# RetNet attention and a SwiGLU FFN on one core: eight attention jobs ahead of all up groups, and two token units that share each rounded weight group

## The chip, the cores and the metric

One core of a Trainium2 chip runs one program. The time is device microseconds (us) of one execution. The kernel before was run again beside each group of experiments and had medians of 1198.7 to 1199.44 us, so medians of different groups can be set side by side. A ratio is the mean time of one kernel's runs over that of the other's of the same rounds, so it is not quite the ratio of the medians that are quoted.

## The reference

Eight sequences of 576 positions, eight heads of 64, go through a retention layer. Its output is the input of an FFN over 4608 tokens. The FFN's weights come as float64.

```python
# attention: q, k, v are (8, 8, 576, 64) float32
scores = scale * np.matmul(q, k.transpose(0, 1, 3, 2))
Dmat = np.where(rel >= 0, gamma[:, None, None] ** rel[None, :, :], 0.0)
attn = np.matmul(scores * Dmat[None, :, :, :], v)
# FFN: x is (4608, 512), w_gate and w_val (512, 1536), w_out (1536, 512)
rms = np.sqrt(np.mean(x * x, axis=-1, keepdims=True) + 1e-06)
xn = x / rms * rms_g
g = xn @ w_gate
out = (g * (1.0 / (1.0 + np.exp(-g))) * (xn @ w_val)) @ w_out
```

## The kernel before

The attention is cut into 32 jobs, one for two heads of one sequence. First q and k of a job are turned, that is, transposed; the 64 positions left over after four blocks of 128 are its tail. TensorE then makes scores and states of a job, VectorE weighs them and sums the states, TensorE makes the values and the part carried over from earlier chunks, and VectorE moves the result into `x`. The FFN works on units of 384 tokens. Of each unit the squares of `x` are summed and averaged and `x` is scaled (the norm), then come the up groups (`w_gate` and `w_val`), then the down projection (`w_out`). The first two units use plain products and the other ten a scheme with fewer multiplications; those ten take most of the time, and the change does not touch them.

The weights are rounded from float64 to float32 on the chip, in 18 chunks of 1 MB. One chunk costs VectorE five instructions and ScalarE three:

```python
def exponent(i):                 # VectorE, then three Relu on ScalarE
    nc.vector.tensor_scalar(out=e, in0=words_of[i][..., 1::2], scalar1=20, ...)
    nc.scalar.activation(out=e.bitcast(F32), in_=e, func=AF.Relu, bias=least)
    ...                          # two more
def mantissa(i):                 # three on VectorE; the third needs e
    ...
def join(i):                     # one on VectorE
    ...
def weights_to(n):               # before: one chunk at a time
    while n_chunks < min(n, len(chunks)):
        mantissa(n_chunks + 1)
        join(n_chunks)
        load_chunks(n_chunks + 4)
        exponent(n_chunks + 2)
        n_chunks += 1
```

The order of the start is what the change is about. The jobs of sequence 0 (0 to 3) are turned by TensorE. The jobs of sequence 1 (4 to 7) are turned by VectorE and stand between the up groups of unit 0. An up group is a pair `(m, g)`: `m` says gate or value, `g` which third of the width; it takes two chunks of weights and is made of four quarters of about 2.6 us.

```python
for j in range(NHP):             # jobs of sequence 0
    slot(j)                      # scores, states, weigh; values and carried of job j - 1
    if j + 1 < NHP:
        turn(j + 1)
    ...                          # a chunk rounded at j == 1 and at j == 2
...
order = [(0, 0, 0), 4, (0, 1, 0), 5, (0, 0, 1), 6, (0, 1, 1), 7, (0, 0, 2)]
order += [(1, 0, 0), (1, 1, 0), (0, 1, 2)]
order += [(1, m, g) for g in (1, 2) for m in range(2)]
for what in order:               # (unit, m, g), or a job of sequence 1
    ...
    weights_to(4 * g + 2 * m + 2)
    for _ in up_plain(u, m, g):
        step += 1
        weights_to(2 + (step + 1) // 2)
```

## Time and profile before

| | us |
|---|---|
| median of 3 runs | 1199.05 (1198.05 to 1199.83) |
| first weighing of a job on VectorE | 18.48 |
| down projection of unit 1 starts on TensorE | 219.72 |
| from there to the end of the span | 981.3 |

The stages of the profiled span of 1201.0 us and the orders of time are in the prediction below. In a stage line the first number after the window is its length, then comes each engine's busy time with its count of instructions, then the clock granted to TensorE (1.00 is full speed), the share of the 16 DMA engines that was busy, and GB/s.

### The profile page before, as it was taken

To read this page: it belongs to the slowest core of one execution; us is meant where nothing else is said; L and a number is where in the kernel's file an instruction comes from. 1 tells how busy PE (TensorE), PEld (TensorE's weight loads), DVE (VectorE), ACT (ScalarE), POOL (GpSimd) and SP (SyncE) were. 2 spreads that over 40 slices of the span, in tenths; PEclk is the share of its full clock that TensorE was granted. 3 is DMA by queue.
4 is the path that set the end of the run, shared out by engine and by line. 5 is a ranking of instruction groups with operands and counts; after the bars stand their busy time and mean duration, and the time that the engine had idled before them with its cause. 6 is when DMAs were issued, how large, how long until landed. Compare 5 with 4: busy or idle time off the path is not lost.

```text
span 1201.0 us, 24041 instructions
## 1 busy us (share of the span) xinstructions
PE 1147.4 (96%) x10184; PEld 1036.7 (86%) x10184; DVE 674.6 (56%) x1370; ACT 244.3 (20%) x468; POOL 44.9 (4%) x74
## 2 busy tenths in 40 slices
PE   3798799999999999999999999999999999999998
PEld 3555455446999999999999999999999999999998
DVE  3888872024775666355566566446556555535442
ACT  4555541011220211220210211120220111120110
POOL 0000004130000000000000000000000000000000
PEclk9698799999999999999999999999999999999999
DMA  9498431021376455306436446405345412403304
GB/s 227 113 217 185 142 131 53 10 65 45 93 212 134 99 130 128 122 2 134 113 82 133 103 108 145 128 1 129 92 109 124 112 55 80 132 1 90 121 1 105
DMA packets 302347, 126.28 MB, mean 105 GB/s; under 512 B 279328, under 2 KB 284832, under 8 KB 302240
## 3 DMA queue, kind: packets, MB, share of 16 engines
q1 hardware_dynamic: 289840, 105.30, 36.5%
q10 hardware_dynamic: 12400, 19.44, 5.0%
q8 instruction: 80, 1.31, 0.5%
q14 instruction: 27, 0.22, 0.1%
HBM read 109.75 MB, written 14.94 MB: 104 GB/s over the span
## 4 chain that ended last, share of the span: by engine, by line
PE 82%; DVE 13%; issue 2%; ACT 1%; DMA 1%; SPq 0%; POOL 0%; DVEq 0%; ACTq 0%; POOLq 0%
PE x L438 13%; PE z L438 13%; PE w L438 13%; PE up L495 7%; PE wo L568 7%; PE y L438 6%; PE out L509 5%; PE xo L568 4%; PE zo L568 4%; PE yo L568 3%; DVE sum L282 2%; PE av L318 1%; DVE sq L378 1%; DVE ret L270 1%; DVE x L333 1%
## 5 line engine op out<-in xcount | busy, mean ns | idle before, releaser
L462 ACT COPY m<-x 128x384 f32<-128x384 f32 x60 | 28.7, 478 | 431.7 <-PE x L438 431.7
L438 PE MATMUL z<-x,w_gate 128*128 128x192 f32 x480 | 89.3, 330 | 2.2 <-DVE sum L282 2.2
L438 PE MATMUL x<-x,w_val 128*128 128x192 f32 x480 | 89.6, 330 | 0.0
L438 PE MATMUL x<-x,w_gate 128*128 128x192 f32 x480 | 88.8, 328 | 0.0
L438 PE MATMUL w<-sums,w_val 128*128 128x192 f32 x480 | 87.8, 326 | 0.0
L438 PE MATMUL z<-x,w_val 128*128 128x192 f32 x480 | 87.8, 326 | 0.0
L438 PE MATMUL w<-sums,w_gate 128*128 128x192 f32 x480 | 87.8, 326 | 0.0
L438 PEld LDWEIGHTS z<-x,w_gate 128*128 128x128 f32 x480 | 80.7, 192 | 2.5 <-DVE sum L282 2.5
L568 PE MATMUL xo<-h,w_out 128*128 128x192 f32 x480 | 82.1, 328 | 0.0
L568 PE MATMUL wo<-h,w_out 128*128 128x192 f32 x480 | 82.0, 328 | 0.0
L438 PEld LDWEIGHTS x<-x,w_val 128*128 128x128 f32 x480 | 79.8, 191 | 0.6
L438 PEld LDWEIGHTS x<-x,w_gate 128*128 128x128 f32 x480 | 79.7, 191 | 0.5
L438 PEld LDWEIGHTS w<-sums,w_gate 128*128 128x128 f32 x480 | 79.6, 190 | 0.0
L438 PEld LDWEIGHTS w<-sums,w_val 128*128 128x128 f32 x480 | 79.6, 190 | 0.0
L438 PEld LDWEIGHTS z<-x,w_val 128*128 128x128 f32 x480 | 79.6, 190 | 0.0
L568 PEld LDWEIGHTS xo<-h,w_out 128*128 128x128 f32 x480 | 78.1, 190 | 0.5
L568 PEld LDWEIGHTS wo<-h,w_out 128*128 128x128 f32 x480 | 78.1, 190 | 0.0
L445 DVE TENSOR_TENSOR u<-m,y 128x384 f32<-128x384 f32 x60 | 32.8, 546 | 79.8 <-PE y L438 79.8
L445 DVE TENSOR_TENSOR h<-u,w 128x384 f32<-128x384 f32 x60 | 33.3, 554 | 75.0 <-PE w L438 75.0
L495 PE MATMUL up<-x,w_gate 128*128 128x384 f32 x192 | 68.2, 515 | 4.0 <-DVE h L501 2.1
L495 PEld LDWEIGHTS up<-x,w_gate 128*128 128x128 f32 x192 | 38.2, 202 | 33.1 <-issue 3.6
L457 ACT ACTIVATE h<-h 128x384 f32<-128x384 f32 x90 | 47.0, 523 | 88.6 <-DVE h L445 88.6
(120 smaller groups left out, 1764.1 us busy)
## 6 DMA issues: line engine op xcount, KB each, us to landing
w_out<-w_blocks SPq DMA_DIRECT2D x70, 768.0 KB, 4.9
k<-in_k_dram SPq DMA_DIRECT2D x64, 128.0 KB, 3.1
v<-in_v_dram SPq DMA_DIRECT2D x64, 128.0 KB, 3.0
qraw<-in_q_dram SPq DMA_DIRECT2D x112, 72.0 KB, 2.7
kraw<-in_k_dram SPq DMA_DIRECT2D x112, 72.0 KB, 2.7
out_dram<-o SPq DMA_DIRECT2D x304, 24.0 KB, 1.6
w_out<-in_moe_w_gate_dram ACTq DMA_DIRECT2D x6, 1024.0 KB, 5.8
w_blocks<-w_out SPq DMA_DIRECT2D x7, 768.0 KB, 5.7
```

The source lines that it names most:

```text
L270: nc.vector.scalar_tensor_tensor(out=ret[:, e], in0=s[:, e, :SC].rearrange("p (c k) -> p c k", k=L), scalar=float(_gamma(H)[2 * hp + e] ** ...
L282: nc.vector.scalar_tensor_tensor(out=t[:, c], in0=t[:, c - 1], scalar=gc[:, hp : hp + 1], in1=part, op0=ALU.mult, op1=ALU.add,)
L318: mm = nc.tensor.matmul(av[odd][side(e), i * L : i * L + L], lhsT=d["sum"][side(e), c - 1], rhs=d["qT"][side(e), c * L : c * L + L], start ...
L333: nc.vector.tensor_tensor(out=x[:, first - c0 // L :: 2], in0=av[odd][:, i * L : (i + n) * L].rearrange("p (c k) -> p c k", k=L), in1=gq[: ...
L378: nc.vector.tensor_tensor(out=sq[a], in0=sq[a], in1=sq[b], op=ALU.add)
L438: nc.tensor.matmul(ps[:, i * HU : i * HU + HU], lhsT=w_up[m][:, 2 * blk + c, cut], rhs=t_of[u][blk][:, c], start=(start and i == c == 0), ...
L445: nc.vector.tensor_tensor(out=o, in0=a, in1=pairs_of(ps), op=ALU.add)
L457: nc.scalar.activation(out=o, in_=c, func=AF.Silu)
L462: nc.scalar.copy(out=s1, in_=pairs_of(x_))
L495: nc.tensor.matmul(ps[:, :U], lhsT=w_up[m][:, 4 * half + c, i * P : i * P + P], rhs=x_of[u][:, c], start=(c == 0), stop=(c == NHP - 1),)
L509: nc.tensor.matmul(ps[:, :DM], lhsT=h_of[u][:, f, s * P : s * P + P], rhs=w_out[:, f], start=(f == 0), stop=(f == NF - 1),)
L568: nc.tensor.matmul(ps[:, i * HU : i * HU + HU], lhsT=w_slots[:, k % 4, c, i * P : i * P + P], rhs=rhs[:, c], start=(start and i == c == 0) ...
```

## The change

The intent: do all eight jobs first, with TensorE turning all of them, and then let both units use a weight group one after the other, so that the rounding of two chunks has the products of two groups on TensorE to hide behind and not of one. The rounding is made a generator, of which one or two steps are taken at a time. Other parts: q comes in runs of 1 KB, the tails of all heads of a sequence in three loads, v is scaled by GpSimd, the Silu table is loaded at once, and the first four chunks are loaded by the sync queue.

```diff
@@ turn
-        scale_v(j)
+        for e in range(2):
+            for t in (d["v"][:, :, e], d["vt"][:, e].unsqueeze(1)):
+                g = gv[: t.shape[0], hp, e : e + 1].unsqueeze(2).to_broadcast(list(t.shape))
+                nc.gpsimd.tensor_tensor(out=t, in0=t, in1=g, op=ALU.mult)
@@ rounding, in steps (each yield ends one)
+    def rounding():
+        ...
+        exponent(0)
+        yield
+        exponent(1)
+        yield
+        yield from mantissa(0)
+        yield
+        for i in range(len(chunks)):
+            if i + 1 < len(chunks):
+                yield from mantissa(i + 1)
+                yield
+            join(i)
+            n_chunks += 1
+            load_chunks(i + 4)
+            yield
+            if i + 2 < len(chunks):
+                exponent(i + 2)
+                yield
@@ start
+        nc.scalar.activation(out=tick, in_=mhalf[:1], func=AF.Silu)
+        load_first(0)
+        load_tails(0)
+        load_first(1)
+        load_first(2)
+        load_chunks(1, nc.sync)
+        ... (tables, turn of job 0)
+        for j in range(2 * NHP):
+            slot(j)
+            if j + 1 < 2 * NHP:
+                turn(j + 1)
+            ... (squares, loads of job j + 2, norm of unit 0, loads of job 8 at j == 5 and 6)
+            load_chunks((1, 2, 2, 3, 3, 4, 4, 4)[j], nc.sync)
+            weights((0, 1, 2, 2, 2, 2, 1, 0)[j])
+        for m, g in [(m, g) for g in range(NG) for m in range(2)]:
+            for u in range(2):
+                weights_to(4 * g + 2 * m + 1)
+                for i, _ in enumerate(up_plain(u, m, g)):
+                    ... (values, carried and norm of unit 1 inside the first group)
+                    weights(2)
+                    if i == 1:
+                        weights_to(4 * g + 2 * m + 2)
+        following(2 * NHP - 1)
         weights_to(len(chunks))
```

## The prediction

> **What bounds the kernel now.** I first read the stages (busy time of each engine between chosen instants), then the order of time of TensorE and VectorE in the first 300 us, then the start on ScalarE. The stages:
>
> ```profile
> core 0: us, PE busy (x) PEld busy (x) DVE busy (x) ACT busy (x) POOL busy (x), PEclk, DMA share, GB/s
> 0.00:22.90 22.90, 9.29 (x210) 7.37 (x211) 4.44 (x18) 7.08 (x18) 0.78 (x7) 1.00 1.01 248
> 22.90:57.00 34.10, 21.14 (x405) 16.86 (x401) 27.81 (x69) 22.73 (x37) 1.13 (x4) 0.69 0.56 133
> 57.00:147.40 90.40, 74.83 (x728) 47.35 (x729) 78.38 (x136) 43.91 (x60) 1.21 (x5) 0.87 0.75 179
> 147.40:219.90 72.50, 72.50 (x225) 42.82 (x226) 34.26 (x43) 21.72 (x27) 15.96 (x12) 1.00 0.23 78
> 219.90:287.00 67.10, 67.10 (x364) 31.74 (x363) 9.93 (x25) 7.73 (x18) 16.10 (x14) 1.00 0.16 41
> 287.00:1201.00 914.00, 902.59 (x8263) 890.61 (x8260) 519.74 (x1083) 141.08 (x310) 9.67 (x32) 1.00 0.40 100
> ```
>
> From 147.4 us on TensorE is never idle except for some 11 us in 914; the change touches nothing there. Before it, TensorE waits: the start (22.9 us), the four jobs of sequence 0 at VectorE's pace (27.81 busy of 34.10), then weight rounding, the four jobs of sequence 1 and five of the twelve up groups, again with VectorE nearly full (78.38 of 90.40). So only the first 219.9 us can move. The other 979 us (1199.05 - 219.9) stay.
>
> TensorE shows what a wait costs and what an up group costs without waits:
>
> ```profile
> start us, us, engine line op out<-in xcount [idle before <-releaser]
> 102.65 0.37 PE L257 MATMUL last<-v,k 64*64 64x64 f32 x2 [3.75 <-ACT h L503]
> ...
> 104.77 12.04 PE L495 MATMUL up<-x,w_val 128*128 128x384 f32 x32
> ...
> 157.80 20.80 PE L495 MATMUL up<-x,w_val 128*128 128x384 f32 x64
> ```
>
> Two groups in 20.80 us, or 72.48 us for the seven from 147.4 to 219.9: 10.35 us a group, 2.59 a quarter of one. After a 3.75 us idle the same group takes 12.04.
>
> VectorE's units of work, from its order of time, are one job and one 1 MB weight chunk:
>
> ```profile
> 34.84 0.88 DVE L270 SCALAR_TENSOR_TENSOR ret<-s,causal 128x320 f32<-128x320 f32 x2
> 35.64 0.21 DVE L280 COPY sum<-s 128x64 f32<-128x64 f32 x1
> 35.89 1.86 DVE L282 SCALAR_TENSOR_TENSOR sum<-sum,gc,s 128x64 f32<-128x64 f32 x6
> 37.85 0.28 DVE L282 SCALAR_TENSOR_TENSOR sum<-sum,gc,last 128x64 f32<-128x64 f32 x1
> 38.05 0.94 DVE L333 TENSOR_TENSOR x<-av,gq 128x192 f32<-128x192 f32 x4
> 38.91 0.68 DVE L707 TENSOR_SCALAR w_val<-w_out 128x1024 uint32<-128x1024 uint32 x1
> 39.63 1.23 DVE L711 SCALAR_TENSOR_TENSOR w_val<-w_out,w_val 128x1024 f32<-128x1024 uint32 x1
> 40.77 1.22 DVE L714 SCALAR_TENSOR_TENSOR w_gate<-w_out,w_gate 128x1024 uint32<-128x1024 uint32 x1
> 41.91 1.22 DVE L722 SCALAR_TENSOR_TENSOR w_gate<-w_gate 128x1024 f32<-128x1024 f32 x1
> 43.16 0.69 DVE L686 TENSOR_SCALAR w_gate<-w_gate 128x1024 uint32<-128x1024 uint32 x1
> ...
> 184.29 1.58 DVE L722 SCALAR_TENSOR_TENSOR w_out<-w_out,w_gate 128x1024 f32<-128x1024 f32 x1
> ```
>
> By start-to-start: weighing a job 3.2 us (34.84 to 38.05), moving it into x 0.86; a chunk is 0.7 + 1.14 + 1.14 + 1.25 + 0.61, about 4.9. The last line is used below. The start on ScalarE:
>
> ```profile
> 13.57 1.28 ACT L199 ACT_TABLE_LOAD   x1 [13.57 <-DMA v<-in_v_dram]
> ```
>
> ScalarE issues the weight loads too; its queue stands until 13.57, so copies of turned q and k that could have begun at 10 to 11 begin at 14.86, and the first weighing at 18.48.
>
> **The Trainium skill.** (1) "TensorE: Matmul & The Clock Gate", Part 1: an idle window of about 3.4 us halves the clock, and about 3.4 us of sustained work restores it. The trace agrees: idles of 3.75 and 4.08 us are followed by a granted 0.50, one of 2.15 us is not. (2) "SBUF — State Buffer", Who interferes with whom: GpSimd and a VectorE instruction with two SBUF inputs exclude each other. The trace of before has one sign of it: the joining instruction takes 1.58 us at 184.29, beside GpSimd's work, and 1.22 elsewhere. (3) "ScalarE: Activation LUTs", What ACT_TABLE_LOAD costs: about 1283 ns for a load; here 1.28 us, twice (13.57 and 51.15). (4) "DMA: Bandwidth & Descriptors", Specifications: runs of at least 512 B for line rate. No row of the before trace isolates it; 2 us slices with weights alone in flight move up to 414 GB/s, slices with 64-float rows about 170.
>
> **The change part by part.**
>
> Start. q comes in runs of 1 KB, one load a job instead of three; the last 64 rows of all heads in three loads; weights are issued later and from the sync queue; the table is loaded at once. The built program gives eight completion semaphores to all loads in turn, so each load waits for the one eight before it: the tails of q and k go out at about 5 to 6 us (loads cost 0.5 to 0.6 us to issue, 2.4 to land unloaded, as q did at 4.07), land at 8.2, and turn, copy, scores and states (1.35 + 1.1 us at the slow clock) put the first weighing W0 at 11.4 instead of 18.48.
>
> Eight jobs. The four stream transposes of q and k of sequence 1 (2 x 0.7 us each job) leave VectorE, and TensorE turns them: about 1.6 us at full clock. v is scaled on GpSimd (estimate 2.1 us a job, from its 1.40 us for 128x512). VectorE carries 3.2 + 0.86 a job, 0.5 for the sum of squares, and ten rounding steps. TensorE's order, though, is a chain: states, carried (1.2), turn (1.6), the tail's two copies and turns behind each other on ScalarE (1.2), values (0.8; half waits for the last sum, because it takes over its bank), scores and states (1.3): 6.1 us a job. So a job takes the larger of 6.1 and VectorE's work. VectorE: job 1 4.7, 2 5.9, 3 6.85, 4 6.4, 5 8.25 (with the norm's 1.0 us wait for GpSimd), 6 7.3. I add 0.5 to 1 for jobs 2 to 6 for exclusion by GpSimd, 3.4 in all, and 6.5 for job 0 at the slow clock. W7 = 11.4 + 6.5 + 6.2 + 6.7 + 7.7 + 7.2 + 9.2 + 7.5 = 62.4.
>
> Between. The first quarter of the first up group hides behind the last weighing. Then values and carried of job 7 (to W7 + 5.5) and one quarter (to 8.1); the next needs chunk 1, which VectorE joins only after the last weighing, two moves and two sums of squares and four rounding steps: W7 + 12. A TensorE idle of 3.8 us. The two quarters after it, the mean and the scale of unit 1 bring its first group to W7 + 19.3, plus 2.5 for the slow clock that such an idle brings (from 12.04 against 10.48, and small work beside it).
>
> Twelve groups. 44 quarters x 2.59 = 113.9. A weight group now serves two units, so TensorE gives 20.7 us for two chunks, whose rounding is 9.8 us of VectorE, plus 4.4 where h is multiplied: VectorE no longer bounds, and steps one or two at a time keep it from standing before h.
>
> Sum: 62.4 + 19.3 + 2.5 + 113.9 = 198.1, against 219.9: 21.8 less, 1177. Without exclusion by GpSimd 1174; with the idle too short for the clock 1171. The second rounding chain, the combination of weights on GpSimd and the output stage stay off the path: rounding ends about 20 us ahead of the last group. I put it at 1175.
>
> **The rivals.** (a) Work is only moved: VectorE keeps the same chunks, and eight jobs in a row leave TensorE half idle for 50 us where it was fed with up groups. That is the reason the gain is 22 us and not 40. For it: 50 us of the new stage at VectorE's pace. Against: the twelve groups then need no wait. If chunks stall them after all (loads go out only as a chunk is joined, and sit behind ScalarE's work), 8 to 15 us come back: 1185 to 1190. (b) Loads bound the eight jobs: 7 MB of q, k, v plus 4 MB of weights in 50 us is 220 GB/s, what the first 30 us moved at 94% of the engines. Only eight loads are in flight. Each job's loads are asked for two jobs ahead, some 12 us, so I expect them hidden; if not, 5 to 10 us: 1180 to 1187. (c) The gate: a TensorE half busy through eight jobs stays at 0.5. Then its 8.7 us of slow work a job is the bound, and 8 to 10 us are added; but that would leave it without idle and so wake it. (d) All of it better: no exclusion, no slow clock, W0 at 10: 1166.
>
> **Range and chances.** 1165 to 1187 holds the sum with any one of these rivals. The 2% line is at 1175.1, on top of my value; slips add rather than cancel, but the sizes of exclusion and clock are the ones I padded. Faster by over 2%: 0.48; within: 0.50; slower: 0.02.
>
> **What would show it right or wrong.** First weighing at 11 to 12 us; weighings of jobs 1 to 7 6 to 9 us apart, the eighth at 57 to 63, with VectorE nearly full between. GpSimd scaling at about 0.7 us for 128x256; joins and mantissas longer than 1.22 us beside it. One TensorE idle of 3 to 4 us after the second quarter of the first group, released by the join, and a granted 0.5 after it. Then none before the down projection, which should start at 194 to 199 instead of 219.9. A DMA named as releaser inside the eight jobs, or waits inside the later groups, would make it wrong; so would a change in the 979 us that follow.

## The result, and the profile after

The changed kernel takes 1186.34 us (median of 4, 1184.56 to 1188.96) against 1199.44 (median of 4). The ratio is 0.9889, 95% interval 0.9863 to 0.9916: about 13 us faster, which is "within 2%". The predicted gain was 24 us.

The stages of the changed kernel, cut at its first weighing, its eighth weighing, the first group of unit 1, the down projection and 67 us later:

```profile
core 0: us, PE busy (x) PEld busy (x) DVE busy (x) ACT busy (x) POOL busy (x), PEclk, DMA share, GB/s
0.00:12.66 12.66, 6.10 (x96) 5.01 (x98) 0.34 (x6) 3.08 (x6) 2.41 (x10) 1.00 0.78 171
12.66:69.73 57.07, 43.69 (x1143) 37.19 (x1144) 42.19 (x117) 19.81 (x40) 16.79 (x36) 0.85 0.74 186
69.73:90.35 20.62, 15.77 (x108) 9.12 (x107) 12.82 (x33) 7.46 (x10) 0.95 (x2) 0.92 0.17 52
90.35:205.94 115.59, 113.87 (x353) 66.87 (x354) 85.11 (x100) 59.77 (x69) 10.49 (x8) 1.00 0.36 119
205.94:273.00 67.06, 67.06 (x361) 31.73 (x361) 11.07 (x27) 7.73 (x18) 21.64 (x19) 1.00 0.36 94
273.00:1186.80 913.80, 901.24 (x8271) 889.18 (x8267) 520.64 (x1083) 141.04 (x310) 9.67 (x32) 1.00 0.41 100
```

The last two lines sum to 980.86 us against 981.28 before, so the whole gain lies ahead of the down projection: it starts at 205.94 and not at 219.72, 13.8 us earlier. In the fourth line TensorE is busy 113.87 of 115.59 us: weight groups shared by two units keep it fed, as intended. The second line is the weak one. The eight jobs take 57.07 us, and no engine is full in it: TensorE 77%, VectorE 74%, DMA 74%. Its clock is 0.85 on average.

TensorE's order of time shows who stops it there. The columns are start, length, engine, line, operation, operands, count, and in brackets the idle time before with its releaser:

```profile
31.18 1.09 PE L201 MATMUL turn_q<-ident,h 128*64 128x128 f32 x16 [1.16 <-DMA h<-in_q_dram]
...
35.01 0.28 PE L209 MATMUL turn_t<-ident,w_val 64*128 64x64 f32 x1 [2.15 <-ACT qT L206]
...
42.03 1.01 PE L334 MATMUL av<-qT,sum 64*64 64x64 f32 x13 [3.79 <-issue]
42.97 1.97 PE L201 MATMUL turn_q<-ident,h 128*64 128x128 f32 x16
...
81.14 4.51 PE L513 MATMUL up<-x,w_gate 128*128 128x384 f32 x8 [3.12 <-DVE w_gate L742]
90.35 10.56 PE L513 MATMUL up<-x,w_gate 128*128 128x384 f32 x32 [0.80 <-DVE x L425]
192.93 13.17 PE L513 MATMUL up<-x,w_val 128*128 128x384 f32 x40 [1.72 <-ACT w_val L521]
```

Five kinds of wait can be seen: a load of q; a copy on ScalarE; 3.79 us in the middle of one job's carried products that nothing in the profile released ("issue"), after which turning q takes 1.97 us and not 1.09 because the clock has halved; and the predicted wait for the join of chunk 1 at 81.14, also followed by slow products (4.51 us for a quarter); and, late in the twelve groups, 1.72 us for ScalarE.

Against the terms of the sum in the prediction:

| term | predicted us | measured us | difference |
|---|---|---|---|
| first weighing | 11.4 | 12.66 | +1.3 |
| eight jobs, first to eighth weighing | 51.0 | 57.1 | +6.1 |
| eighth weighing to unit 1's first group | 21.8 | 20.6 | -1.2 |
| to the down projection | 113.9 | 115.6 | +1.7 |
| down projection starts | 198.1 | 205.94 | +7.9 |

The profiled run is the slowest of the four (span 1186.8, the others 1182.4 to 1184.3), so some of the 7.9 is chance. The question for the chip is the second term.

### The profile page after: what moved, and what is told of

It is laid out like the page before. It is cut to its first block, busy times and chain, and to the rows that moved or that the text cites. A ratio compares the mean times of both kernels' runs of the same rounds, so it can differ in the third digit from the quotient of the medians.

```text
span 1186.8 us, 24268 instructions
## 1 busy us (share of the span) xinstructions
PE 1147.7 (97%) x10320; PEld 1039.1 (88%) x10320; DVE 672.2 (57%) x1362; ACT 238.9 (20%) x452; POOL 62.0 (5%) x106
## 3 DMA queue, kind: packets, MB, share of 16 engines
q8 instruction: 81, 1.33, 0.5%
## 4 chain that ended last, share of the span: by engine, by line
PE 78%; DVE 11%; ACT 5%; DMA 3%; issue 2%; SPq 1%; POOL 0%; DVEq 0%; POOLq 0%; ACTq 0%
PE x L456 13%; PE z L456 13%; PE w L456 13%; PE wo L586 7%; PE y L456 6%; PE out L527 5%; PE xo L586 4%; PE zo L586 4%; PE yo L586 3%; PE up L513 2%; DVE sum L298 2%; PE av L334 2%; ACT w_gate L708 1%; ACT w_gate L709 1%; ACT w_gate L712 1%
## 5 line engine op out<-in xcount | busy, mean ns | idle before, releaser
L513 PE MATMUL up<-x,w_gate 128*128 128x384 f32 x192 | 65.2, 498 | 4.9 <-DVE w_gate L742 3.1
L513 PE MATMUL up<-x,w_val 128*128 128x384 f32 x192 | 62.7, 487 | 1.7 <-ACT w_val L521 1.7
```

The source lines that it names most:

```text
L513: nc.tensor.matmul(ps[:, :U], lhsT=w_up[m][:, 4 * half + c, i * P : i * P + P], rhs=x_of[u][:, c], start=(c == 0), stop=(c == NHP - 1),)
```

## The experiments

Twelve kernels ran. "Stage" below is the time from the first weighing to the eighth. I began with theory A: the stage is long because VectorE and GpSimd exclude each other more than I had allowed, and because of the late chunk 1. The rivals were chance, the loads, and ScalarE's order.

### 1. The changed kernel again

No edit.

> The changed kernel, unaltered, profiled once more. Theory A: the eight-job stage is longer than sized because of fixed causes (VectorE and GpSimd exclude each other, the late chunk 1, the load queue), so the eighth weighing starts at 69 to 70 us again and the time is 1185 to 1188. Rival B: TensorE's 3.79 us stop inside the carried products of job 3, which nothing in the profile released, and the slow clock after it come by chance: then it is absent or elsewhere, the eighth weighing starts at 65 to 67 us and that run is 3 to 4 us shorter.

Measured: 1188.05 us (4 runs, 1184.9 to 1190.45; ratio to the kernel before 0.991). The profiled run has its eighth weighing at 67.34 and a stage of 54.8 us. TensorE stops at the same instruction again, 13 products before the end of job 3's carried part, but for 2.19 us. So the stop is fixed in its place and varies in length; neither theory had that. The kernels below that are the same up to the eighth weighing had stages of 59.0 and 56.0 us with stops of 3.83 and 2.21 us there. One stage therefore means little by itself: four profiles of one code span 54.8 to 59.0, mean 56.7.

### 2. v scaled by ScalarE

```diff
-        for e in range(2):
-            ... nc.gpsimd.tensor_tensor(out=t, in0=t, in1=g, op=ALU.mult)
+        scale_v(j)
```

> One part undone: v is scaled on ScalarE again (1.67 us a job there by the profile of the kernel before), not on GpSimd. Theory A (exclusion by GpSimd is under-sized): the mantissa steps fall back to 1.22 us and the scale of the unit to 0.68, the eight-job stage is 3 to 5 us shorter and so is the time, 1181 to 1184. Rival C (ScalarE's order, copies of turned q and k behind other work, is what TensorE waits for): 1.7 us a job more on ScalarE lengthens the stage by 3 to 8 us, 1189 to 1194. If the two cancel, or neither is on the path: within 1 us of the unaltered kernel.

Measured: 1185.23 us (0.989). The groups of VectorE between 12 and 67 us show what GpSimd costs it. The columns are line, operands, count, busy us and mean ns, and idle time before with releasers. First the changed kernel, run again:

```profile
L730 DVE SCALAR_TENSOR_TENSOR w_gate<-w_out,w_gate 128x1024 f32<-128x1024 uint32 x2 | 3.0, 1493 | 0.0
...
L395 DVE TENSOR_TENSOR sq<-sq,sq 128x384 f32<-128x384 f32 x4 | 2.2, 559 | 4.6 <-ACT sq L387 4.6
```

and with v on ScalarE:

```profile
L727 DVE SCALAR_TENSOR_TENSOR w_gate<-w_out,w_gate 128x1024 f32<-128x1024 uint32 x2 | 2.4, 1222 | 0.0
...
L392 DVE TENSOR_TENSOR sq<-sq,sq 128x384 f32<-128x384 f32 x4 | 2.2, 559 | 7.8 <-ACT sq L384 7.7
```

The mantissa steps are back at 1.22 us, and VectorE's busy time in the stage falls from 42.19 to 39.56 us. But it now waits 7.8 us for squares from the busier ScalarE where it waited 4.6. The stage is 54.6 us, at the lower edge of the spread of the unaltered code (54.8 to 59.0), and the time lies between theory A and no change. So exclusion is real and worth 2.6 us of VectorE (my allowance was 3.4), yet it does not explain the missing 6 us.

### 3. No rounding steps in the jobs

```diff
-            weights((0, 1, 2, 2, 2, 2, 1, 0)[j])
+            weights(0)
```

> No rounding step inside the eight jobs; the loads of weights stay where they are. VectorE loses 12.3 us of its work there, ScalarE 6 to 9 us. Theory A (VectorE and what stands behind rounding set the stage): jobs follow each other at 6.1 us or less, the eighth weighing starts at 55 to 58 instead of 69.7; what is left undone (some 12 us of VectorE before chunk 0 is joined) then comes after the jobs, so that the first up group starts 8 to 12 us after it otherwise would and the total is about the same, 1184 to 1192. Rival D (loads or instruction supply set the stage): the eighth weighing still starts at 64 or later, with idle time released by DMA or by nothing, and the total is 1195 or more.

Measured: 1201.54 us (1.0025). The stage of this kernel:

```profile
12.71:66.26 53.55, 42.69 (x1142) 36.03 (x1142) 32.20 (x106) 13.29 (x34) 13.29 (x36) 0.87 0.79 198
```

VectorE's busy time fell by 10 us, to 60% of the stage, and the stage is still 53.55 us. Theory A falls: VectorE's work alone does not set the stage. The total is 13 to 15 us longer, because the rounding not done here is done after the jobs: from the eighth weighing to unit 1's first group it takes 39.97 us and not 20.62.

### 4. Chunk 1 asked for at the start

```diff
-        load_chunks(1, nc.sync)
+        load_chunks(2, nc.sync)
...
-            load_chunks((1, 2, 2, 3, 3, 4, 4, 4)[j], nc.sync)
+            load_chunks((2, 2, 2, 3, 3, 4, 4, 4)[j], nc.sync)
```

> Weight chunk 1 is asked for at the start together with chunk 0, ahead of job 3's loads, so that it lands long before VectorE's step needs it at 28.7 us. Theory A: VectorE's 1.52 us wait for it goes, the three Relu of its exponent run earlier, the two copies for job 4 aren't stuck behind them (TensorE waited 2.15 us there): the gap from the third to the fourth weighing falls from 7.7 to about 6.2 and the time by 1 to 2 us, 1184.5. Rival E (the early 1 MB delays q, k and v of jobs 1 to 3, which share the DMA engines): the first three weighings are 1 to 3 us later and the total is the same or up to 2 us longer.

Measured: 1185.29 us (0.9883). VectorE's wait is gone and the third gap is 6.1 us, as theory A had it; but the first three weighings come at 13.59, 19.40 and 26.85 and not at 12.66, 17.53 and 23.74, as rival E had it, and the eighth at 69.78. Part of that is spread: in the four profiles of the unaltered code the first three lie at 12.53 to 13.00, 17.53 to 18.54 and 23.74 to 26.15, and the third gap at 6.8 to 7.7. The run agrees with a load moved forward being paid for by the loads it overtakes, and so points to the loads as a whole; it does not show it.

### 5. No steps and no weight loads

The same with `load_chunks((0, 0, 0, 0, 0, 0, 0, 4)[j], nc.sync)` and without the load at the start.

> The kernel without rounding steps in the eight jobs, and now without weight loads in them too; chunks 0 to 3 are asked for after the last job. With the steps gone but the loads kept the eighth weighing started at 66.3 us, hardly before the unaltered 67.3 and 69.7, so VectorE's steps don't set the stage. Theory L (loads set it: the 4 MB of weights keep the DMA engines full, so that q, k, v and the blocks of instructions land late): without weight loads the eighth weighing starts at 52 to 58, no stop of TensorE over 1.5 us without a releaser, clock at full through most of the stage. Rival C (TensorE's and ScalarE's chain of a job sets it, whatever is loaded): still 63 to 67. The total is far longer in both, since the rounding then starts after the jobs: 1205 to 1220.

Measured: 1194.3 us (2 runs, 0.9962). The stage:

```profile
12.85:57.57 44.72, 37.18 (x1142) 31.37 (x1142) 32.37 (x106) 13.37 (x34) 13.90 (x36) 1.00 0.74 178
```

Theory L holds: the same code of the engines, with 4 MB fewer to load, takes 44.72 and not 53.55 us, and the clock stays at 1.00. Of the 8.8 us between the two stages, 5.5 are TensorE's own busy time (42.69 and 37.18 us for as many products, at clocks of 0.87 and 1.00) and only 3.3 are idle time. One sign of theory L failed: a stop of 1.83 us without a releaser is left (see the section on the stop). I had expected 1205 to 1220 for the total and it is 7 us faster than with the loads in place. From the eighth weighing to unit 1's first group it takes 40.43 us, where the run with loads took 39.97: with no rounding among the jobs, the four chunks cost next to nothing after them and 8.8 us among them.

### 6. All of unit 0, then all of unit 1

```diff
-        for m, g in [(m, g) for g in range(NG) for m in range(2)]:
-            for u in range(2):
+        for u in range(2):
+            for m, g in [(m, g) for g in range(NG) for m in range(2)]:
```

> One part undone: after the eight jobs all six groups of unit 0 are computed, then all six of unit 1, so a weight group serves 10.4 us of TensorE again instead of 20.8. My step was: two chunks cost VectorE 9.8 us plus 2.2 for the products of h, 12.0 a group, against 10.4 on TensorE, so VectorE bounds unit 0 and some 1.6 to 2.5 us are lost in each of five groups, and each late group may let the clock fall: 8 to 15 us longer than the unaltered kernel, 1195 to 1201. Rival R (rounding is far enough ahead, the alternation only moves the waits): within 3 us of the unaltered kernel, 1185 to 1190.

Measured: 1249.97 us (1.0422). That is 64 us longer, not 8 to 15, so a mechanism is at work that I had not counted. Between 90 and 200 us VectorE is busy for only 52.57 of 110 us. Three orders of time show a ring. TensorE waits for VectorE's join:

```profile
121.82 6.86 PE L513 MATMUL up<-x,w_gate 128*128 128x384 f32 x16 [4.61 <-DVE w_gate L742]
```

ScalarE waits for TensorE's product to make the Silu, and only then starts the three Relu of the next exponent, which stand behind it in its order:

```profile
126.13 0.49 ACT L521 ACTIVATE h<-up 128x384 f32<-128x384 f32 x1 [6.76 <-PE up L513]
126.52 1.14 ACT L708 ACTIVATE w_gate<-w_gate,least 128x1024 f32<-128x1024 uint32 x1
```

and VectorE waits for those Relu in the last mantissa step, ahead of the next join:

```profile
130.05 1.23 DVE L734 SCALAR_TENSOR_TENSOR w_gate<-w_out,w_gate 128x1024 uint32<-128x1024 uint32 x1 [5.70 <-ACT w_gate L712]
```

One turn of the ring gives one chunk, which feeds two quarters, and takes some 11.8 us (TensorE resumes at 97.34, 109.17, 121.82, 132.47, 144.33). At full clock the two quarters are 5.2 us of products; here they take 6.9 to 8.4, since the clock falls in the waits (0.78 on average from 90 to 200 us). Ten such turns, up to 210 us, make about the 64 us. With two units a chunk feeds four quarters, and rounding gets ahead. So rounding in steps as it stands here pays only with a group shared between units. Whether sharing would pay without the steps was not run.

### 7. Weights and job 8 later

```diff
-            load_chunks((1, 2, 2, 3, 3, 4, 4, 4)[j], nc.sync)
+            load_chunks((1, 2, 2, 2, 2, 3, 3, 4)[j], nc.sync)
@@ join of chunk 0 no longer loads; the loads of job 8 move behind the up groups
```

> Chunks 2 and 3, which no step needs before the jobs are over, are asked for two to four jobs later, and the loads for job 8 after the up groups. Theory L (loads set the stage): less traffic between 30 and 62 us, TensorE's stop in job 3 falls from 2 to 4 us to under 1.5, q of job 4 lands in time, the eighth weighing starts at 60 to 64, and the time is 4 to 7 us shorter, 1180 to 1183. Rival C (ScalarE's and TensorE's chain): eighth weighing at 66 to 69, the time as before within 1.5 us. If chunk 2 or 3 comes too late for its rounding, a wait of some us at the second up group takes the gain back.

Measured: 1184.86 us (0.9886), a stage of 53.65 us, the eighth weighing at 66.77. TensorE's longest stop without a releaser is 1.31 us. The direction is theory L's, the size is not: 1.5 to 3 us of the 4 to 7 expected. The eighth weighing is where rival C had it (66 to 69), so this run alone does not decide between the two. VectorE now waits 2.34 us for chunk 1 and 1.51 for squares, so another wait took part of the gain.

### 8. Chunk 1 joined before chunk 2's mantissa

```diff
-            if i + 1 < len(chunks):
+            if i + 1 < len(chunks) and i != 1:
                 yield from mantissa(i + 1)
                 yield
             join(i)
@@ and for i == 1 the mantissa of chunk 2 after it
```

> Chunk 1 is joined before the three mantissa steps of chunk 2 instead of after them: VectorE gives the third quarter of the first up group its weights some 3.6 us earlier. TensorE's 3.12 us wait there goes, and with it the half clock after it (the quarter then took 4.51 us instead of 2.59). Expected: 4 to 5 us shorter than the unaltered kernel, 1181.5 to 1182.5. Rival: another wait takes its place (the sums of squares or the scale of unit 1, which also stand in VectorE's order): 0 to 2 us shorter, 1184.5 to 1186.5.

Measured: 1183.61 us (0.9868). Its eighth weighing is at 68.97, and unit 1's first group follows 15.92 us later where it was 20.62:

```profile
84.89 10.56 PE L513 MATMUL up<-x,w_gate 128*128 128x384 f32 x32 [0.80 <-DVE x L425]
```

TensorE's wait of 3.12 us and the slow quarter after it are gone, 4.7 us in the trace. The medians fell by 2.7 and 4.4 against the two measurements of the changed kernel, and 1183.61 lies between the expectation and its rival.

### 9. Steps kept, one chunk loaded (wrong result on purpose)

```diff
+        if i == 1:
+            words_of[1] = words_of[0]
+            return
@@ chunks 2 and 3 after the jobs; the tenth step (exponent of chunk 2) left out
```

> A wrong result on purpose: the rounding steps stand in the eight jobs as in the changed kernel (nine of the ten), but only chunk 0 is loaded there; the steps of chunk 1 work on chunk 0's words, and chunks 2 and 3 are asked for after the jobs. It fills the missing cell of a table of two causes: with steps and loads the eight jobs took 54.8 to 57.1 us from the first weighing to the eighth, with loads alone 53.6, with neither 44.7. Theory L (loads alone set the stage): 46 to 49. Theory T (two bounds of nearly one length stand side by side, VectorE's order with its steps and the loads; taking one away leaves the other): 51 to 54.

Measured: 1183.22 us (2 runs), result wrong as intended. The stage:

```profile
12.78:63.70 50.92, 40.85 (x1126) 34.55 (x1128) 42.21 (x115) 20.17 (x40) 16.45 (x36) 0.93 0.75 188
```

| stage, us | weights loaded | not loaded |
|---|---|---|
| with rounding steps | 54.8 to 59.0, mean 56.7 (4 profiles) | 50.9 (chunk 0 loaded, nine steps) |
| without | 53.6 | 44.7 |

Neither expectation fits whole: 50.9 lies above L's 46 to 49 and just under T's 51 to 54. Loads cost 5.8 us with the steps there and 8.8 without, steps 3.1 with the loads and 6.2 without. Together they cost 12.0: each hides part of the other. Apart from the first cell these are single profiles.

### 10 to 12. Put together

The first version joins 2 (v on ScalarE), 7 and 8, and takes no step after the first quarter of unit 0's last value group, where I took VectorE's wait for the last chunk to stand.

> A version put together from what the runs showed: chunk 1 joined before chunk 2's mantissa (alone 3 to 4 us), chunks 2 and 3 and job 8's loads later (alone 1 to 2 us), v on ScalarE again (alone 1 to 3 us), and no rounding step in the quarter where VectorE stood 3.83 us for the last chunk (1.7 us of TensorE's wait). If they add, 7 to 9 us less than the changed kernel: 1178 to 1181. If v on ScalarE and the later loads relieve the same wait: 1180 to 1183.

Measured: 1175.57 us (1175.0 to 1177.4; ratio to the kernel before 0.98, 0.9787 to 0.9813): 11 to 12 us less than the changed kernel, a little more than the parts one by one give in sum (5.3 to 10.4 against its two measurements). Whether it is over 2% faster than the kernel before is unclear: the interval has 2% inside it. TensorE's stop of 1.78 us before the last five quarters was still there, so the hold was in the wrong place.

> The same, and the tails of q and k of the first sequence asked for ahead of v of job 0 (TensorE waited 1.7 and 0.95 us for them), and the exponent of chunk 1 taken after the mantissa of chunk 0, a job later, so that VectorE doesn't stand for chunk 1. If the first weighing comes 1 to 2 us earlier and the gap from the third weighing to the fourth falls to 7: 1 to 3 us less than the former, 1176 to 1179. If the loads' order sets the pace all the same: no difference.

Measured: 1178.2 us (0.9814), not better. The first weighing came at 12.17 and not 12.52, and the gap from the third to the fourth was 8.2 us (7.8 in the first version), since TensorE now waited there for VectorE (1.54 and 1.38 us). Spread: 1175.31 to 1180.84.

The last run holds the rounding two quarters earlier:

```diff
-                    weights(2)
+                    weights((2, 0, 0, 0)[i] if (m, g, u) == (0, 2, 1) else 2)
```

> The first put-together version once more with the hold of the rounding put where it has to be. In it the 1.78 us stop of TensorE ahead of the last five quarters was still there, so my place for it was wrong: the step that waits 3.9 us for the last chunk stands two quarters earlier in the program, in the last gate group of unit 1, and the last two Silu of that group stand on ScalarE behind its three Relu. Now no step is emitted after the last three quarters of that group. If this is the cause, the two Silu run at once, the 1.78 us stop is gone, all else is equal, and the time is 1173.3 to 1174.3. If the stop is only moved (the products of h now wait): 1175 to 1176.

Measured: 1175.52 us (6 runs, 1173.64 to 1177.15; ratio to the kernel before 0.9797, 0.9785 to 0.981, so again unclear at 2%). Its stages:

```profile
13.15:64.88 51.73, 40.58 (x1143) 33.82 (x1144) 39.45 (x116) 28.36 (x68) 1.64 (x8) 0.97 0.81 204
64.88:80.83 15.95, 14.03 (x108) 8.38 (x107) 12.81 (x33) 7.47 (x10) 0.94 (x2) 1.00 0.21 67
80.83:194.43 113.60, 113.60 (x353) 66.96 (x354) 85.03 (x100) 59.79 (x69) 8.13 (x6) 1.00 0.36 121
```

In the third line TensorE is busy for all of 113.60 us: the stop is gone, and its cause is shown (two Silu of unit 1 stood on ScalarE behind Relu that waited for the last chunk). The median did not move against the first version: the first weighing was 0.6 us later and the part after the down projection 979.2 and not 977.5 us, which differs by some 4 us between profiles anyway. This version and the first beat both kernels; which of the two is faster isn't settled.

### TensorE's stop that nothing released

The trace of the changed kernel around it:

```profile
22.44:38.24 15.80, 11.18 (x382) 9.64 (x380) 11.11 (x33) 10.37 (x16) 4.97 (x12) 1.00 0.93 243
38.24:42.03 3.79, 0.00 (x1) 0.00 (x0) 3.72 (x7) 0.00 (x0) 2.41 (x3) 0.83 0.99 277
42.03:49.90 7.87, 7.37 (x126) 6.10 (x127) 4.32 (x13) 1.92 (x5) 1.36 (x3) 0.50 0.37 90
```

In the stop the DMA engines are 99% busy, most of the packets with short rows:

```profile
DMA packets 2282, 1.06 MB, mean 278 GB/s; under 512 B 1868, under 2 KB 2124, under 8 KB 2281
```

Between the idle at 22.44 and this stop TensorE issued 762 instructions (382 products and 380 weight loads), and from there to the next such idle, which begins at 49.90, another 253 (126 and 127). The Trainium skill, "Runtime: NRT & Kernel Launch", Instruction fetch mechanics, says that instructions are fetched in blocks of 16 KiB, 256 instructions, over a DMA queue of the sequencer's own. The counts are close to three blocks and one, and the profile lists 81 packets of 1.33 MB on an instruction queue, 16.4 KB each. So the stops may sit where a new block is needed. That is argued from counts and not shown: by the same count two blocks ended between 22.44 and 38.24 without a stop of over 0.3 us, and in the stop shown an instruction packet is recorded at about 39 us, well ahead of its end. Nor does the data traffic explain the lengths. At this place the stop is only 1.04 us without weight loads. But at the next place (49.90 in the first profile) TensorE stopped for 2.10 us in the second profile of the changed kernel, with the DMA engines 39% busy in the stop, and for 1.83 us without weight loads, with 38%:

```profile
49.95 0.39 PE L273 MATMUL s<-v,k 64*64 64x64 f32 x11 [2.10 <-issue]
43.03 0.39 PE L273 MATMUL s<-v,k 64*64 64x64 f32 x11 [1.83 <-issue]
```

And the first combined version has no stop over 0.57 us in the whole stage, though its stage moves more (204 GB/s against 186). What makes the stops, and what sets their length, stays open.

## Why the prediction was right or wrong

The class was right and the time lies in the range, at its upper edge; the centre was 11 us too low (the sum itself gave 1177). Part of this is luck: the class had a chance of 0.50 against 0.48, and the second measurement of the same kernel, 1188.05 us, lies just above the range.

- **Where it can move.** Right. The part after the down projection changed by 0.4 us.
- **Start.** Nearly right: 12.66 for 11.4. The tails landed later than assumed (TensorE waited 1.67 and 0.95 us for those of q and k).
- **Eight jobs.** This is the step that failed. The prediction took "the larger of 6.1 and VectorE's work" for a job and said of the loads "so I expect them hidden". Measured 57.1, on average 56.7, for 51.0. With three of the four chunks out of the way the stage is 50.9, so what the sum left out is the loads among the jobs: 5.8 us beside the steps, on single profiles apart from the first mean (so that 50.9 meets 51.0 may be chance). Rival (b) had the size, "5 to 10 us: 1180 to 1187", but not the path. TensorE waited for a load by name for only 1.16 us in the first profile and nowhere in the second; of the 5.8 us, some 3.4 are longer busy time of TensorE (44.2 us on average and 40.85) at a lower clock. The chain was sized well: with neither steps nor loads a job takes 6.4 us (44.72 over seven) for 6.1. GpSimd's exclusion was about right too (2.6 for 3.4) and not what was missing.
- **Clock.** Rival (c) came in part: 0.85 on average, not 0.5 throughout. With neither loads nor steps it is 1.00. In the first profile it halves at the long stop (0.50 from 42.03 to 49.90 us). In the second it was 0.50 from 36 to 38 us already, before the stop and after the 2.17 us wait for a copy, so stops are not its only cause. The predicted halving in the first group came after an idle of 3.12 us.
- **Between.** Right in mechanism and in size: an idle of 3.12 us released by the join (3.8 predicted) and slow products after it, 20.6 us for 21.8. Experiment 8 took it away and got 4.7 us back.
- **Twelve groups.** Nearly right: 115.6 for 113.9. The one stop, 1.72 us, is ScalarE's order behind the last chunk. But the reason given, VectorE's sum of 9.8 and 4.4 us, is only half of it. Experiment 6 shows that without sharing the ring of joins, products and Relu costs 64 us, though VectorE is half idle.
- **Its own signs.** Most failed: the eighth weighing at 69.73 (57 to 63), two weighings 11 us apart (6 to 9), VectorE 74% busy in the jobs (nearly full), the down projection at 205.94 (194 to 199). Two things that "would make it wrong" came: a DMA as releaser inside the jobs (1.16 us) and a wait inside the later groups (1.72 us). The idle released by the join, and the slow clock after it, came as written.

## What to carry to other kernels

Work moved to the start of a kernel shares its window with every load that is wanted there: before trusting that a load asked for two jobs ahead is hidden, sum all loads of the window and ask which of them need come in it. Where two causes nearly fill the same time, taking one away shows little; test them together. A helper engine that works in order closes a ring when the work that feeds the next step stands behind the result of the present one, and such a ring is found in waits, not in busy shares.

## What the Trainium skill lacked or had wrong

- "Runtime: NRT & Kernel Launch", Instruction fetch mechanics: "The cost of crossing a 16 KiB boundary is one DMA tail-bump, mostly hidden." If the stops above are such crossings, which is argued and not shown, some were not hidden: TensorE stopped for 2.2 to 3.8 us at one place in all four profiles of the same code, with the DMA engines 99% busy in the one shown, and for 2.10 us at the next place in one of them, with 39%. Of causes that make a fetch late the page names only the taken branch.
- "SBUF — State Buffer", Who interferes with whom, gives the exclusion but no cost in a mixed stage: here 16.8 us of GpSimd work beside VectorE added 2.6 us to VectorE's 39.6.
- I found no page with the cost of ScalarE's order in such a ring: 11.8 us a turn for what is 5.2 us of products at full clock.
